# A fused attention and gated feed-forward kernel: wider PSUM regions, a copied hidden layer and a written-out order of work

## The chip, the cores and the metric

The kernel runs on one core of one Trainium2 chip. Its time is the device time of one execution in microseconds (us); lower is better. A core has TensorE (PE, matmuls; PEld are its weight loads), VectorE (DVE), ScalarE (ACT), GpSimd (POOL), and SyncE (SP), whose queue issues nearly all DMAs here. Each engine works through its own list of instructions in the order in which the program issues them, and waits there on semaphores for the others.

## The reference

Attention with a cluster mask, then a feed-forward layer (FFN), in float32:

```python
# q, k, v: (4 batches, 8 heads, 768 tokens, 64); centroids: (8, 16, 64)
q_assign = argmax(q_n @ c_n.T); k_assign = argmax(k_n @ c_n.T)   # nearest centroid, vectors normalised
mask = q_assign[:, :, :, None] == k_assign[:, :, None, :]
scores = where(mask, q @ k.T / 8, -1e9)
x = softmax(scores) @ v                       # as (3072 tokens, 512)
h = x @ w_in                                  # (3072, 1024)
e = exp(h - max(h)); solu = h * e / sum(e)
ln = (solu - mean(solu)) / sqrt(var(solu) + 1e-6) * g_ln
out = ln @ w_out                              # (3072, 512)
```

## The kernel before

**Attention.** The work is cut into 16 pairs of heads (4 batches by 4 pairs). For a pair, q and k are loaded (`load`, `load_tokens`), turned so that the head dimension lies on partitions (`turn` on DVE at L326; in batch 0 `turn_tokens` on PE at L303 and a copy), and cast into `qbig` and `kbig` (`cast`, L332 to L336). `clusters` (L346) multiplies with the centroids; `turn_back`, `assign_max`, `assign_hot` and `assign_turn` (DVE, L353 to L368) make one-hot rows, and `place` (L375, eight copies a pair) puts them beside the head dimension of `qbig` and `kbig`. With these rows a score gets 256 added where the clusters agree, so one exponential with a bias of -256 does mask and softmax numerator at once.

A unit is 256 (query, head) rows against 768 keys: 96 units in all, 24 a batch. Its scores fill three PSUM banks of 512 columns (`scores`, L458); each bank is exponentiated by one ACT instruction (`expo`, L463). Twelve matmuls (`values`, L475) multiply the result with v and a column of ones; `normalise` (L487, L498) divides. In batches 0 to 2 the units of a head follow one another for the first three pairs, and the last pair goes by blocks of 256 queries; a block of 128 tokens is complete for the FFN only when the last pair has reached it.

**FFN.** There are 24 blocks f of 128 tokens. For each: `turn_x` (a transposing DMA on SP, L506), `f_h` (eight matmuls, L539), `f_max` and `f_neg` (DVE, L546, L550), `f_exp` (two ACT instructions that read PSUM, L557), `f_u` (two DVE products e times h that read PSUM, L563), `f_turn` (transposing DMA), `f_bn` and `f_aggr` (DVE, L574, L578), `f_alpha` (four small POOL instructions, L584 to L590), `f_y` (eight matmuls, L600), `f_scale` (L606, L608), `f_out`. Before this, w_in is cast on POOL (L408), and w_out is summed over its rows and centred on DVE (L425 to L437).

**PSUM.** Scores have three banks in a ring, h three, the attention output one, everything else one. A bank of h is held until its product `f_u` is done.

**Order.** `Weave` holds every operation with an engine, a cost and a key, and `run` plays a list scheduler at build time: it takes the ready operation with the smallest key at the earliest time, and the instructions are issued in that order. `AWAY` moves single operations to another engine.

Of the kernel before, what the change touches and what calls it, by code (L numbers as in the profile page):

```python
# [13 lines left out]
AXY = mybir.AxisListType.XY  # L14
# [7 lines left out]
class Weave:  # L22
# [3 lines left out]
    FEED_KINDS = "tx ptx tu ptu hm h ng ex u bn ag al y sc ou".split()  # L26
    PAIR_KINDS = "ld tp xa xt ca lv cv cl tb mx oh ot pl bl".split()
    FEED = [-1, 2, 2.5, 4.5, 5, 4, 6.5, 11, 18, 7.5, 8, 12.5, 7.5, 21, 10, 15.5, 16.5, 10.5,
        4.5, 7.5, 1.5, 0.5, 2.5, -0.5]
    PAIR = [-27, 0, 1.5, -6, -9, -4.5, 0, -3, 19.5, -7.5, 1.5, -3, 21, 13.5, 21, 19.5]  # L30
    KIND = {'cv': -23.5, 'wi': -36.0, 'tb': -12.0, 'ca': 16.0, 'xa': 20.0, 'N': -1.0, 'tp':
        38.0, 'lg': 36.5, 'lo': -4.0, 'pl': -3.0, 'bl': 11.5, 'z': 35.5, 'xt': -1.0, 'lv': 1.5,
        'ce': -1.0, 'oh': -1.0, 'su': 0.5, 'ld': 5.0, 'li': 4.0, 'ot': -1.0, 'cl': 0.5, 'mx':
        0.5}
    AWAY = {}
    AWAY.update(dict.fromkeys("""
        ca0.0.1.0 ca0.0.1.1 ca0.1.0.0 ca1.1.1.0 ca1.2.1.0 ca1.3.0.1 ca2.1.0.0 ca2.1.0.1
        ca2.2.0.1 ca2.3.0.0 ca3.3.0.1 xa0.0.0 xa0.2.0 xa0.2.1 xt0.2.0 xt0.2.1 xt0.3.1
    """.split(), "ACT"))
    AWAY.update(dict.fromkeys("""  # L40
        bl3.2 bl3.3 pl0.0.0.1.0 pl0.0.0.1.1 pl0.0.1.1.0 pl3.0.0.1.1 pl3.2.0.0.0 pl3.2.0.1.0
        pl3.3.0.1.0 sc15 sc17 sc22
    """.split(), "DVE"))
    AWAY.update(dict.fromkeys("""
        bl0.0 ca0.0.0.0 ca0.0.0.1 pl0.0.0.0.0 pl0.0.0.0.1 pl0.0.1.0.0 pl0.0.1.0.1
        pl0.2.1.0.1 pl0.2.1.1.1
    """.split(), "POOL"))

    HOP = 0.17
    EPS = 0.12  # L50
    AHEAD = 2
    DEPTH = 4.0

    def __init__(self):
        self.ops, self.by = [], {}

    def add(self, name, eng, cost, key, fn, needs=(), after=(), take=None, give=None, move=0.0,
            bulk=False, lag=(0.5, 0.6)):
        assert name not in self.by, name
        key += self.later(name)  # L60
        self.by[name] = len(self.ops)
        self.ops.append(dict(name=name, eng=eng, cost=cost, key=key, fn=fn, needs=list(needs),
                             after=list(after), take=take, give=give, move=move,
                             bulk=bulk, lag=lag))

    def later(self, name):

        kind, rest = re.fullmatch(r"([A-Za-z]+)(.*)", name).groups()
        if kind in self.FEED_KINDS:
            return self.FEED[int(rest.split(".")[0])]  # L70
        if kind in self.PAIR_KINDS:
            b, p = rest.split(".")[:2]
            return self.PAIR[4 * int(b) + int(p)] + self.KIND.get(kind, 0)
        return self.KIND.get(kind, 0)

    def run(self):
        ops, by = self.ops, self.by
        n = len(ops)
        users = [[] for _ in range(n)]
        left = [0] * n  # L80
        for i, o in enumerate(ops):
            o["n"] = [by[x] for x in o["needs"]]
            o["a"] = [by[x] for x in o["after"]]
            left[i] = len(o["n"]) + len(o["a"])
            for j in o["n"] + o["a"]:
                users[j].append(i)
        start, end = [None] * n, [None] * n
        free, tokens, bus = {}, {}, 0.0
        ready = {}
        floor = [0.0] * n  # L90

        def open_(i):
            o = ops[i]
            floor[i] = max([end[j] + (self.HOP if ops[j]["eng"] != o["eng"] else 0.03)
                            for j in o["n"]] + [start[j] for j in o["a"]] + [0.0])
            ready.setdefault(o["eng"], []).append(i)

        for i in range(n):
            if not left[i]:
                open_(i)  # L100
        order = []
        while len(order) < n:
            best = None
            for e, lst in ready.items():
                t0 = free.get(e, 0.0)
                cand = []
                for i in lst:
                    tk = ops[i]["take"]
                    at = max(t0, floor[i])
                    if ops[i]["move"]:  # L110
                        at = max(at, bus - (self.AHEAD if ops[i]["bulk"] else self.DEPTH))
                    if tk is not None:
                        held = tokens.get(tk, 0.0)
                        if held is None:
                            continue
                        at = max(at, held + self.HOP)
                    cand.append((at, i))
                if not cand:
                    continue
                lo = min(c[0] for c in cand)  # L120
                at, i = min((c for c in cand if c[0] <= lo + self.EPS),
                            key=lambda c: (ops[c[1]]["key"], c[1]))
                if best is None or at < best[0]:
                    best = (at, i, e)
            at, i, e = best
            o = ops[i]
            ready[e].remove(i)
            start[i] = at
            free[e] = at + o["cost"]
            end[i] = at + o["cost"]  # L130
            if o["move"]:
                bus = max(end[i] + o["lag"][0], bus) + o["move"]
                end[i] = bus + o["lag"][1]
            if o["take"] is not None:
                tokens[o["take"]] = None
            if o["give"] is not None:
                tokens[o["give"]] = end[i]
            order.append(i)
            for j in users[i]:
                left[j] -= 1  # L140
                if not left[j]:
                    open_(j)
        self.start, self.end, self.order = start, end, order
        for i in order:
            ops[i]["fn"]()
# [3 lines left out]
def kernel(  # L149
# [25 lines left out]
    FF2 = 512  # L175
    n_ff2 = d_ff // FF2
    VS, VW = D + 2, D + 1

# [3 lines left out]

    const = ctx.enter_context(tc.tile_pool(name="const", bufs=1))
    big = ctx.enter_context(tc.tile_pool(name="big", bufs=1))
    wst = ctx.enter_context(tc.tile_pool(name="wst", bufs=4))
    ld = ctx.enter_context(tc.tile_pool(name="ld", bufs=8))
    xtp = ctx.enter_context(tc.tile_pool(name="xtp", bufs=6))
    pr = ctx.enter_context(tc.tile_pool(name="pr", bufs=3))
    vp = ctx.enter_context(tc.tile_pool(name="vp", bufs=3))
    ep = ctx.enter_context(tc.tile_pool(name="ep", bufs=9))  # L190
    mo = ctx.enter_context(tc.tile_pool(name="mo", bufs=2))
    sm = ctx.enter_context(tc.tile_pool(name="sm", bufs=4))
    ps_s = ctx.enter_context(tc.tile_pool(name="ps_s", bufs=3, space=bass.MemoryType.PSUM))
    ps_h = ctx.enter_context(tc.tile_pool(name="ps_h", bufs=3, space=bass.MemoryType.PSUM))
    ps_o = ctx.enter_context(tc.tile_pool(name="ps_o", bufs=1, space=bass.MemoryType.PSUM))
    ps_m = ctx.enter_context(tc.tile_pool(name="ps_m", bufs=1, space=bass.MemoryType.PSUM))
# [5 lines left out]
    def on(name, engine):  # L202
        return wv.AWAY.get(name, engine)

    R = 6
    qbig = [big.tile([P, 2, S], BF16, name=f"qbig{i}") for i in range(R)]
    kbig = [big.tile([P, 2, S], BF16, name=f"kbig{i}") for i in range(R)]
    v1 = [big.tile([P, 2, n_t, VS], BF16, name=f"v1_{i}") for i in range(R)]

    def slot(b, p):  # L210
        return (b * n_pair + p) % R

    def behind(b, p, what):

        i = b * n_pair + p - R
        if i < 0:
            return []
        b0, p0 = divmod(i, n_pair)
        ns = sorted({where[b0, 2 * p0 + hh, su] for hh in range(2) for su in range(n_t)})
        return [f"{what}{n}.{k}" for n in ns for k in range(n_k if what == "S" else 2)]  # L220

    SRC, DST = (q, k), (qbig, kbig)

    def rows(h):
        return slice(0, D) if h % 2 == 0 else slice(D, P)

    def hot_rows(hh):
        return slice(D, D + NB) if hh == 0 else slice(0, NB)

    def used(h):  # L230
        return slice(0, D + NC_) if h % 2 == 0 else slice(0, P)

    n_first = 2
    UNITS, GROUPS = [], []
    for b in range(B):
        if b < B - 1:
            for p in range(n_pair):
                a, c = 2 * p, 2 * p + 1  # L240
                if p < n_pair - 1:
                    hs = [[(h, s2) for s2 in range(n_t // 2)] for h in (a, c)]
                else:
                    hs = [[(a, s2), (c, s2)] for s2 in range(n_t // 2)]
# [40 lines left out]
    def by_token(b):  # L285

        return b < n_turned
# [665 lines left out]
```

## Time and profile before

| | |
|---|---|
| runs | 242.68, 243.94, 244.36 us; median 243.94 |
| span of the profiled execution | 238.8 us, 5.1 below the median |
| TensorE clock granted | 1.000 |
| PE, DVE, ACT, POOL busy | 219.9, 206.8, 204.9, 142.8 us |
| DMA | 38.61 MB |

The profile gives the profiled execution's span, from its first to its last instruction, and not its time; the runs' times include some 5 us around it. A busy time counts the union of the intervals in which an instruction is under way. Since a matmul is shown from issue to its last result, and the next one starts before that, PE's busy time is more than its work. For that the distance between the starts of instructions that follow one another without a wait is the better measure; it is called the pitch below.

### The profile page before, as it was taken

The page shows a single profiled execution, that of the slowest core. Times are in us where ns is not written, and L with a number is a line of the kernel's source. Part 1 is how long each engine was busy: PE and PEld are TensorE (multiplying, and loading weights), DVE is VectorE, ACT ScalarE, POOL GpSimd, SP SyncE. Part 2 cuts the span into 40 slices and gives each one's busy share as a digit, 9 for nine tenths or more (in the row PEclk, how much of TensorE's full clock was granted, in tenths as well). Part 3 has the DMA queues.
Part 4 walks back from the last instruction along what each step waited for, and adds up shares of the span by engine and source line. Part 5 has one row for each costly group of instructions (what it writes and reads, how often), then busy time and mean ns, then how long its engine had stood idle before and what let it go on. Part 6 is the DMA issues. An engine that isn't in the chain of part 4 may idle for free.

```text
span 238.8 us, 6759 instructions
## 1 busy us (share of the span) xinstructions
PE 219.9 (92%) x2384; PEld 147.5 (62%) x2384; DVE 206.8 (87%) x427; ACT 204.9 (86%) x428; POOL 142.8 (60%) x328
## 2 busy tenths in 40 slices
PE   0969999999999999899899999999999999999983
PEld 0646775675655667666566677657667776747441
DVE  4468699999999899999899999998979779999991
ACT  2569998999788999999899999988989998969461
POOL 4983888996075386898948648898802510310331
PEclk9999999999999999999999999999999999999999
DMA  7999988988599898989789989873535154558422
GB/s 203 273 275 219 255 306 226 183 123 180 98 156 202 166 221 166 207 169 212 138 179 180 204 144 165 214 186 96 69 88 50 48 113 110 72 152 154 91 88 88
DMA packets 133217, 38.61 MB, mean 162 GB/s; under 512 B 124472, under 2 KB 128576, under 8 KB 133184
## 3 DMA queue, kind: packets, MB, share of 16 engines
q1 hardware_dynamic: 131616, 37.80, 76.9%
q10 hardware_dynamic: 1568, 0.39, 0.7%
q8 instruction: 18, 0.29, 0.5%
q14 instruction: 15, 0.12, 0.2%
HBM read 23.11 MB, written 6.29 MB: 123 GB/s over the span
## 4 chain that ended last, share of the span: by engine, by line
PE 63%; DVE 10%; ACT 8%; POOL 7%; issue 6%; DMA 5%; ACTq 0%; DVEq 0%; POOLq 0%
PE sps L458 17%; PE yps L600 14%; PE hps L539 14%; PE ops L475 11%; ACT e L463 6%; PE csc L346 4%; DMA xT<-x 2%; DVE w_out_c L437 2%; PE tps L303 2%; DMA uT<-u 2%; DVE hm L546 2%; POOL kbig L336 1%; DVE qbig L375 1%; POOL qbig L334 1%; ACT e_sb L557 1%
## 5 line engine op out<-in xcount | busy, mean ns | idle before, releaser
L463 ACT ACTIVATE e<-sps 128x512 bf16<-128x512 f32 x288 | 148.8, 624 | 10.7 <-PE sps L458 10.1
L458 PE MATMUL sps<-qbig,kbig 80*128 80x256 bf16 (+3 forms) x648 | 101.5, 262 | 5.4 <-POOL qbig L375 2.2
L458 PEld LDWEIGHTS <-kbig 80*128 80x128 bf16 (+1 forms) x648 | 58.5, 121 | 24.6 <-issue 9.9
L475 PEld LDWEIGHTS <-e 128*128 128x128 bf16 x1152 | 57.2, 98 | 20.5 <-issue 3.8
L475 PE MATMUL ops<-v,e 128*128 128x65 bf16 x1152 | 65.5, 194 | 1.0 <-DVE x L498 0.6
L539 PE MATMUL hps<-w_in_sb,xT 128*128 128x512 bf16 x192 | 53.2, 379 | 1.4 <-DMA xT<-x 0.7
L600 PE MATMUL yps<-w_out_c,uT 128*128 128x512 bf16 x184 | 45.4, 379 | 1.1 <-DVE qbig L375 0.7
L557 ACT ACTIVATE e_sb<-hps,nmax 128x512 bf16<-128x512 f32 x48 | 32.9, 700 | 3.1 <-DVE nmax L550 3.1
L546 DVE TENSOR_REDUCE hm<-hps 128x1 f32<-128x512 f32 x48 | 31.9, 676 | 3.2 <-PE hps L539 2.8
L563 DVE TENSOR_TENSOR u<-e_sb,hps 128x512 bf16<-128x512 bf16 x48 | 31.7, 679 | 2.7 <-ACT e_sb L557 2.5
L375 POOL COPY kbig<-oht 32x192 f32<-32x192 f32 x57 | 20.9, 366 | 21.8 <-DVE oht L368 19.5
L574 DVE BATCH_NORM_STATS2 bs<-u 128x6 f32<-128x512 bf16 x48 | 31.6, 678 | 0.0
L600 PEld LDWEIGHTS <-uT 128*128 128x128 bf16 x192 | 17.9, 98 | 17.7 <-DMA uT<-u 1.2
L336 POOL TENSOR_SCALAR kbig<-xt 64x768 bf16<-64x768 f32 x28 | 23.4, 837 | 2.7 <-DVE xt L313 1.3
L334 POOL CAST qbig<-xt 64x768 bf16<-64x768 f32 x25 | 21.5, 860 | 5.5 <-ACT xt L311 4.5
L539 PEld LDWEIGHTS <-xT 128*128 128x128 bf16 x192 | 17.1, 97 | 10.4 <-issue 1.1
L588 POOL TENSOR_TENSOR esq<-esq,mv 128x1 f32<-128x1 f32 x24 | 4.6, 192 | 30.1 <-DVE mv L578 29.1
L326 DVE STREAM_TRANSPOSE xt<-raw 128x768 f32<-128x768 f32 x24 | 22.1, 950 | 0.1
L375 POOL COPY qbig<-oht 32x192 f32<-32x192 f32 x50 | 18.8, 376 | 2.6
L498 DVE TENSOR_TENSOR x<-ops,den 128x384 bf16<-128x384 f32 (+1 forms) x37 | 18.6, 504 | 1.3
L606 ACT ACTIVATE y<-yps,alpha 128x512 f32<-128x512 f32 x20 | 13.9, 695 | 5.7 <-POOL alpha L590 2.9
L389 POOL CAST v<-vf 128x384 bf16<-128x384 f32 x32 | 16.3, 534 | 3.9 <-DMA vf<-in_v_dram 3.4
(75 smaller groups left out, 191.9 us busy)
## 6 DMA issues: line engine op xcount, KB each, us to landing
vf<-in_v_dram SPq DMA_DIRECT2D x16, 384.0 KB, 4.2
out_dram<-y SPq DMA_DIRECT2D x24, 256.0 KB, 2.3
raw<-in_q_dram SPq DMA_DIRECT2D x48, 96.0 KB, 3.6
raw<-in_k_dram SPq DMA_DIRECT2D x48, 96.0 KB, 2.7
w_st<-in_moe_w_in_dram SPq DMA_DIRECT2D x4, 512.0 KB, 5.6
w_g<-in_moe_w_out_dram SPq DMA_DIRECT2D x4, 512.0 KB, 8.0
raw<-in_q_dram SPq DMA_DIRECT2D x7, 192.0 KB, 4.1
raw<-in_k_dram SPq DMA_DIRECT2D x7, 192.0 KB, 4.4
```

The source lines that it names most:

```text
L334: nc.gpsimd.tensor_copy(dst[r, hh, :], xt[r])
L336: nc.gpsimd.tensor_scalar(dst[r, hh, :], xt[r], scalar1=inv_C, scalar2=1.0, op0=Alu.mult, op1=Alu.mult)
L375: (nc.vector if e == "DVE" else nc.gpsimd).tensor_copy(dst, src)
L458: nc.tensor.matmul(sps_[n, k][:, c0:c0 + w], kbig[z][u, h % 2, keys], qbig[z][u, h % 2, q0:q0 + w])
L463: nc.scalar.activation(es[n, k][:], sps_[n, k][:], Act.Exp, scale=exp_scale, bias=-exp_scale)
L475: nc.tensor.matmul(opss[g][:, s, :VW], es[n, k][:, c0:c0 + P], v1[slot(b, h // 2)][:, h % 2, kt, :VW], start=(kt == 0), stop=(kt == n_t - 1))
L539: nc.tensor.matmul(ff[f, "h", f2][:], xTs[f][:, dc, :], w_in_sb[:, dc, f2 * FF2:(f2 + 1) * FF2], start=(dc == 0), stop=(dc == n_dc - 1))
L546: nc.vector.tensor_reduce(ff[f, "hm"][:, f2:f2 + 1], ff[f, "h", f2][:], axis=AX, op=Alu.max)
L557: nc.scalar.activation(ff[f, "e"][:, f2, :], ff[f, "h", f2][:], Act.Exp, bias=ff[f, "nmax"][:], accum_out=ff[f, "esum"][:, f2:f2 + 1])
L563: nc.vector.tensor_tensor(ff[f, "u"][:, f2, :], ff[f, "e"][:, f2, :], ff[f, "h", f2][:], op=Alu.mult)
L574: nc.vector.bn_stats(ff[f, "bs"][:, f2, :], ff[f, "u"][:, f2, :])
L600: nc.tensor.matmul(ff[f, "y"][:], ff[f, "uT"][:, fc, :], w_out_c[:, fc, :], start=(fc == 0), stop=(fc == n_fc - 1))
```

## The change

It is a rewrite of most of the kernel; the arithmetic is that of before. In words:

- Batch 0: pair 0 goes first, all of it; then blocks of 256 queries of the other three pairs follow one another. Its tokens are loaded as (partition, six tokens), one DMA a tensor and pair, and the output rows are written accordingly.
- The eight PSUM banks are fixed tiles: two regions of two banks for scores (`sb`), two banks for h (`hb`), one each for `ob` and `mb`. Two units form a stretch of 3072 columns, cut into regions of 1024; a region gets one exponential. The first two units keep 512. 147 exponentials take the place of 288.
- `f_max` copies -h from PSUM to SBUF and gathers its minimum in the same instruction, bank by bank; `f_neg` is gone. `f_exp` is one ACT instruction of 1024 columns and `f_u` one product of 1024 columns, both from SBUF; the last f keeps halves. 18 of the 24 products, and half of the last, go to POOL.
- From pair 2 on, one-hot rows are made for two pairs at once, and `place` writes them for both heads of both pairs: 40 instructions in place of 128. Nine are on ACT, ten on DVE. Pair 0 is done in two halves.
- The row sum of w_out goes to PE (eight matmuls in column tiles and one to fold); its centring is split between POOL and DVE.
- `f_scale` is on DVE for ten f instead of three.
- `Weave.run` issues the names in `ORDER`, a fixed list of 1,610, in place of the scheduler.

```diff
-                    key=lambda c: (ops[c[1]]["key"], c[1]))
...
+ORDER = """
+ld0.0.0 lg ld0.0.1 ld0.1.0 ld0.1.1 cx cy cz cp tp0.0.0.0 xa0.0.0 cb tp0.0.0.1 gt tp0.0.1.0 lv0.0
+ld0.2.0 ld0.2.1 ld0.3.0 ld0.3.1 gk xt0.0.0 xa0.0.1 cl0.0 ca0.0.0.0.0 ca0.0.1.0.0 tb0.0 mx0.0 oh0.0
+ot0.0 pl0.0.1.0 ca0.0.1.1.0 tp0.0.1.1 tp0.1.0.0 xt0.0.1 xa0.1.0 ca0.0.1.1.1 cl0.0.1 pl0.0.0.1
+tb0.0.1 pl0.0.0.0 tp0.1.0.1 xt0.1.0 tp0.1.1.0 xa0.1.1 tp0.1.1.1 xt0.1.1 cl0.1 ca0.0.0.0.1
...
+        for name in ORDER:
+            o = self.ops[name]
...
+            o["fn"]()
...
+AWAY.update(dict.fromkeys("""
+    ca0.0.0.0.0 ca0.0.0.1.1 ce1 ce5 ce7 pl0.0.1.1 u1.0 u11.0 u12.0 u13.0 u14.0 u15.0 u16.0
+    u18.0 u19.0 u2.0 u21.0 u22.0 u23.1 u3.0 u4.0 u5.0 u6.0 u7.0 u8.0
+""".split(), "POOL"))
...
+    sb = [psum.tile([P, 2, BANK], F32, name=f"sb{i}") for i in range(2)]
+    hb = psum.tile([P, 2, BANK], F32, name="hb")
+    ob = psum.tile([P, BANK], F32, name="ob")
+    mb = psum.tile([P, BANK], F32, name="mb")
...
+        if b == 0:
+            for s2 in range(n_t // 2):
+                side(b, 0, s2)
+            for s2 in range(n_t // 2):
+                for p in range(1, n_pair):
+                    side(b, p, s2)
...
+            w = BANK if n < 2 * n_fine else 2 * BANK
...
+        nc.scalar.activation(es[r][:, :w], src, Act.Exp, scale=exp_scale, bias=-exp_scale)
...
-        nc.vector.tensor_reduce(ff[f, "hm"][:, f2:f2 + 1], ff[f, "h", f2][:], axis=AX, op=Alu.max)
...
+        nc.vector.tensor_scalar(ff[f, "h"][:, f2 * BANK:(f2 + 1) * BANK], hb[:, f2], scalar1=-1.0,
+                                scalar2=nmax[:, f2 - 1:f2] if f2 else 3.0e38, op0=Alu.mult,
+                                op1=Alu.min, accum_out=nmax[:, f2:f2 + 1])
...
+        nc.scalar.activation(ff[f, "e"][:, cols(f, f2)], ff[f, "h"][:, cols(f, f2)], Act.Exp,
+                             bias=ff[f, "nmax"][:, n_ff2 - 1:], scale=-1.0,
+                             accum_out=ff[f, "esum"][:, f2:f2 + 1])
...
+        (nc.vector if e == "DVE" else nc.gpsimd).tensor_tensor(
+            ff[f, "u"][:, cols(f, f2)], ff[f, "e"][:, cols(f, f2)], ff[f, "h"][:, cols(f, f2)],
+            op=Alu.mult)
...
+        src = (asg[t, "oht"][r, :w * L].bitcast(F32).rearrange("p (g s) -> p g s", g=w)
+               .unsqueeze(2).to_broadcast([NB, w, 2, L // 2]))
+        dst = big_[D:HOT, pp:pp + w, :, c0 + x * L:c0 + (x + 1) * L].bitcast(F32)
...
+    def sum_w_out(x):
+
+        for c in range(4):
+            fc = 4 * x + c
+            nc.tensor.matmul(hb[c * NB:(c + 1) * NB, 1], g_wide[:, fc, :], w_g[:, fc, :],
+                             start=(x == 0), stop=(x == n_fc // 4 - 1),
+                             tile_position=(0, c * NB))
```

In `ORDER`, S and E are scores and exponential of a region, V the values of half a unit, N the division, h, hm, ex, u, tu, y, sc, ou the steps of an FFN block, ld and lv loads, ca and cv casts, cl, tb, mx, oh, ot, pl the steps of the one-hot rows. E40 is about the 25th unit's last exponential.

More of the change, by code (lines that the diff above doesn't have):

```diff
@@ L61, in add @@
[L61 to L74, printed above, removed]
@@ L76, in run @@
-    def run(self):
[L77 to L121, printed above, removed]
-                            key=lambda c: (ops[c[1]]["key"], c[1]))
[L123 to L145, printed above, removed]
@@ L222 @@
[L222 to L228 removed]
+        return AWAY.get(name, engine)
+    sb = [psum.tile([P, 2, BANK], F32, name=f"sb{i}") for i in range(2)]
+    hb = psum.tile([P, 2, BANK], F32, name="hb")
+    ob = psum.tile([P, BANK], F32, name="ob")
+    mb = psum.tile([P, BANK], F32, name="mb")
+    R2, R = 3, 6
+    qbig = [big.tile([HOT, 2, 2, S], BF16, name=f"qbig{i}") for i in range(R2)]
```

1132 lines of the change are left out of this document (665 added, 467 removed).

## The prediction

> **What bounds the kernel now.** First the page: span and busy shares.
>
> ```profile
> span 238.8 us, 6759 instructions
> ...
> PE 219.9 (92%) x2384; PEld 147.5 (62%) x2384; DVE 206.8 (87%) x427; ACT 204.9 (86%) x428; POOL 142.8 (60%) x328
> ```
>
> PE is busy for 92% of the span, but its busy time counts overlaps, so I take its work by pitch. The timeline of PE shows stretches without a wait (start, duration, instructions):
>
> ```profile
> 121.83 1.89 PE L600 MATMUL yps<-w_out_c,uT 128*128 128x512 bf16 x8
> 123.56 0.38 PE L458 MATMUL sps<-qbig,kbig 80*128 80x256 bf16 x2
> ...
> 123.97 0.61 PE L458 MATMUL sps<-qbig,kbig 80*128 80x256 bf16 x4
> 124.42 0.35 PE L475 MATMUL ops<-v,e 128*128 128x65 bf16 x6
> 124.61 1.46 PE L539 MATMUL hps<-w_in_sb,xT 128*128 128x512 bf16 x6
> 125.91 0.62 PE L458 MATMUL sps<-qbig,kbig 80*128 80x256 bf16 x4
> ```
>
> ```profile
> 26.46 0.85 PE L346 MATMUL csc<-xt,c_bd 128*32 128x384 f32 x8
> 27.25 0.36 PE L475 MATMUL ops<-v,e 128*128 128x65 bf16 x6
> ...
> 28.30 0.49 PE L303 MATMUL tps<-ident_f,raw 128*128 128x128 f32 x3
> 28.63 0.38 PE L458 MATMUL sps<-qbig,kbig 80*128 80x256 bf16 x2
> ```
>
> Eight FFN matmuls of 512 columns take 123.56 - 121.83 = 1.73 us (0.216 each), four score matmuls of 256 columns 0.45, six value matmuls 0.19, the eight of `clusters` 0.79, three transposes 0.33. With the counts of the groups of instructions:
>
> ```profile
> L458 PE MATMUL sps<-qbig,kbig 80*128 80x256 bf16 (+3 forms) x648 | 101.5, 262 | 5.4 <-POOL qbig L375 2.2 <-ACT e L463 0.9
> ...
> L475 PE MATMUL ops<-v,e 128*128 128x65 bf16 x1152 | 65.5, 194 | 1.0 <-DVE x L498 0.6 <-ACT e L463 0.2
> ...
> L539 PE MATMUL hps<-w_in_sb,xT 128*128 128x512 bf16 x192 | 53.2, 379 | 1.4 <-DMA xT<-x 0.7 <-DVE w_out_c L437 0.5
> ```
>
> 288 banks of 512 score columns are 288 x 0.225 = 64.8; values 1152 / 6 x 0.19 = 36.5; h and as many for y 384 x 0.216 = 83.1; 16 `clusters` 12.6; 48 transposes 5.3; the rest about 2.2. **PE's work is 204.5 us, so 34.3 of the span is idle.** Where? The stages, cut at the first exponential, near the first FFN matmul and at the last scores (columns: stage, length, busy time and count of PE, PEld, DVE, ACT, POOL, clock, DMA share, GB/s):
>
> ```profile
> 0.00:14.15 14.15, 6.32 (x34) 4.45 (x35) 7.47 (x26) 4.61 (x7) 10.02 (x32) 1.00 0.98 241
> 14.15:57.50 43.35, 40.85 (x522) 28.42 (x521) 36.80 (x75) 41.38 (x84) 35.09 (x56) 1.00 0.93 223
> 57.50:220.00 162.50, 158.90 (x1752) 108.25 (x1750) 149.43 (x301) 150.72 (x321) 92.27 (x224) 1.00 0.78 146
> 220.00:238.80 18.80, 13.84 (x85) 6.41 (x82) 13.07 (x29) 8.15 (x18) 5.42 (x18) 1.00 0.32 96
> ```
>
> and PE's groups of the first two stages together:
>
> ```profile
> L458 PE MATMUL sps<-qbig,kbig 80*128 80x256 bf16 (+1 forms) x156 | 28.0, 271 | 4.1 <-POOL qbig L375 2.2
> L475 PE MATMUL ops<-v,e 128*128 128x65 bf16 x298 | 17.2, 194 | 0.6 <-DVE x L498 0.6
> L303 PE MATMUL tps<-ident_f,raw 128*128 128x128 f32 x48 | 8.5, 313 | 0.0
> L346 PE MATMUL csc<-xt,c_bd 128*32 128x384 f32 x48 | 6.8, 549 | 0.0
> ```
>
> That is 156 x 0.1125 + 298 x 0.0317 + 48 x 0.11 + 6 x 0.79 + 1.2 = 38.2 us of work in 57.5. Before the first exponential there are at most 14.15 - 6.3 = 7.8 us of busy-time idle; by pitch some 10. So the second stage has some 9 idle, the third 162.5 - (204.5 - 38.2 - 13.8) = 10.0, the last at least 18.8 - 13.8 = 5.0. The second stage is ACT's: 41.4 of 43.35 busy, and PE has no FFN work to fill in, since its first such matmul starts at 58.2:
>
> ```profile
> L539 PE MATMUL hps<-w_in_sb,xT x192: 376/379/390, 58.2 to 227.5; 128*128 128x512 bf16 x192
> ```
>
> The granted clock is 1.00 throughout. In the third stage PE is at 98% and ACT at 93%, DVE at 92%; it is PE's, with ACT and DVE close behind. **An edit pays only where it takes PE idle time away.**
>
> **PE's work after** is 204.5 plus the row sum of w_out: eight f32 matmuls in column tiles, like two `clusters` widened from 384 to 512 columns, 2 x 0.79 x 512 / 384 = 2.1. The fold stands for the old mean. So 206.6.
>
> **Start.** The chain that ended last opens so (start, us, what):
>
> ```profile
> 5.60 0.48 PE cps L659
> ...
> 8.63 1.75 PE csc L346 x8
> ...
> 14.15 3.53 ACT e L463 x7
> ```
>
> From the norms' end at 5.60 to the first exponential are 8.55 us: transposes, `clusters`, four DVE steps, placing. The new list does these steps for half of pair 0's tokens, which at half the width would save near half of the roughly 4.1 that `clusters` and the DVE steps take. But ahead of S0.0 it also puts the transposes of pair 1: nine half-tensor transposes (0.33), three `clusters` (two of half size) and the centroids', 5 us of PE. From 5.6 that gives 11.0 if no load is late, and 14.15 if the loads of pair 1 eat the gain. I take E0 at 12.0, nearer the first, since the PE rows are known and only the loads are not.
>
> **Second stage, E0 to E40** (about 25 units; before, PE had done 156 / 2 = 78 banks of scores, 26 units, at 57.5). ACT's rows:
>
> ```profile
> 90.70 3.03 ACT L463 ACTIVATE e<-sps 128x512 bf16<-128x512 f32 x6
> 93.57 0.75 ACT L606 ACTIVATE y<-yps,alpha 128x512 f32<-128x512 f32 x1
> ```
>
> ```profile
> L463 ACT ACTIVATE e<-sps 128x512 bf16<-128x512 f32 x288 | 148.8, 624 | 10.7 <-PE sps L458 10.1 <-PE ops L475 0.2
> ...
> L557 ACT ACTIVATE e_sb<-hps,nmax 128x512 bf16<-128x512 f32 x48 | 32.9, 700 | 3.1 <-DVE nmax L550 3.1
> ...
> L332 ACT ACTIVATE qbig<-xt 64x768 bf16<-64x768 f32 x7 | 5.9, 845 | 0.1
> ```
>
> Six exponentials take 93.57 - 90.70 = 2.87, a pitch of 0.478. One of 1024 isn't shown. It costs at most two, 0.956, and at least what 768 columns do, 0.845 less the 0.146 by which 0.624 lies over its pitch, so 0.70. Between 512 and 768 columns the duration rises by 0.863 ns a column; 0.478 + 512 x 0.863 = 0.92, which I take. The Trainium skill (ScalarE: Activation LUTs, What ACT_TABLE_LOAD costs) gives 186 ns plus 0.833 ns a column, less 93 where instructions follow one another: 0.520 for 512, where this trace has 0.478, and 0.946 for 1024. By it the stage is 0.9 longer, an estimate.
>
> Counting the list between E0 and E40: ACT 6 x 0.478 + 34 x 0.92, two FFN exponentials (each two of 0.57 less one start, about 1.1) and seven small ones of about 0.5, 39.7. PE 74 score halves, 47 halves of a unit's values, 13 half-banks of h, four `clusters`, seven transposes and the w_out sum, 39.4. DVE and POOL come to 37 and 34. So where ACT alone was full, two engines are now level, and PE carries 45.1 us of work by E40 against 38.2 before. Before, the stage had 84 ACT instructions: some 77 exponentials, 36.8, and seven others of about 0.53, so 40.5 of 43.35, and the coupling cost 2.9; with two level engines I take 4.3 (0 if the list fits, 8 if as much is lost as PE's idle now). **E40 at 12.0 + 39.7 + 4.3 = 56.0**, with 6.9 more PE work behind it.
>
> **Third stage.** ACT loses 0.036 for each of 107 more exponentials, 3.9, and per FFN block about 0.2; seven `f_scale` go to DVE. On DVE and POOL:
>
> ```profile
> L546 DVE TENSOR_REDUCE hm<-hps 128x1 f32<-128x512 f32 x48 | 31.9, 676 | 3.2 <-PE hps L539 2.8
> L563 DVE TENSOR_TENSOR u<-e_sb,hps 128x512 bf16<-128x512 bf16 x48 | 31.7, 679 | 2.7 <-ACT e_sb L557 2.5
> ...
> L408 POOL CAST w_in_sb<-w_st 128x1024 bf16<-128x1024 f32 x4 | 4.1, 1036 | 0.1
> ...
> L608 DVE TENSOR_SCALAR y<-yps,alpha 128x512 f32<-128x512 f32 x3 | 2.2, 749 | 0.5 <-POOL esq L588 0.5
> ```
>
> ```profile
> L375 POOL COPY kbig<-oht x57: 337/343/807, 12.9 to 188.2; 32x192 f32<-32x192 f32 x57
> ...
> L375 DVE COPY qbig<-oht x14: 247/252/1207, 13.1 to 186.5; 32x192 f32<-32x192 f32 x14
> ```
>
> DVE loses 48 products of 0.679, 32.6, and keeps five and a half of 1024; at twice the row, 7.5. The copy with minimum is nearest to L608 (f32 from PSUM, a scalar per partition), 0.749 against 0.676 for the reduction: plus 3.5. Seven more scalings add 5.2. Net 16 fewer, and the w_out sum goes besides. POOL loses most of its copies: 18 wide ones of 768 columns take the place of 72 of 192 at 0.343. A wide one costs at most four narrow ones, 1.37, and at least three quarters of the cast of 1024, 0.78; I take 0.85, near the row that is nearest in width. Against it stand 18 and a half products of 1024 with two inputs. The trace has no such POOL instruction: at least one pass as the cast of 1024, 1.04; at most two passes, 2.07. I take 1.6. The list from E40 to E120 then has PE 106.0, ACT 97.7, DVE 88, POOL 82, so PE's neighbours move away. I take the third stage's idle of 10.0 for PE waiting on their results, and half of it, 5.0, to stay (2 to 10.0). The tail keeps its order (h, y and the last block's chain), 5.0.
>
> The Trainium skill (GPSIMD Engine Reference, Elementwise) says that a GpSimd product of two tensors takes about 2.6 cycles an element at 1.2 GHz; that is 2.2 us here, an estimate, and it puts POOL at 88.7 in that stretch, still under PE. No run here shows it; by it rival 2 below would need 21 us of waits instead of 23, and I would give it 0.12 instead of 0.10.
>
> **New waits.** h has two banks instead of three, but each comes free after one DVE pass, where it was held through reduction, exponential and product; behind `f_max` stand DVE's transposes and `normalise`, and PE's next h. The copy goes to a staging tile of which there are three, so `f_max` of block f now waits for the product of f - 3, which is mostly POOL's. A score region waits for the exponential two regions back; between these lies one exponential, 0.92, for 0.45 of score matmuls, so ACT is fed as long as PE holds no more than about 0.4 of other work in between; before, two exponentials of 0.478 lay there. On SP a transpose of u waits for POOL's product, and the loads behind it in the list wait along. The front half of the last product pair goes by DVE, the rear by POOL: at most one pass of 512 more in the tail, 0.4.
>
> A further edge of moving `f_u` is the DVE copies: the same copy took 247 ns at best and 1207 at worst beside POOL work. With longer POOL instructions such stretches could reach 2 us, for some 20 DVE instructions whose inputs are all in SBUF, 20 us at most if every one lost half a stretch; with 16 us and the w_out sum off DVE I leave it at nothing on the path.
>
> **The sum.** 56.0 + (206.6 - 45.1) + 5.0 + 5.0 = **227.5 us of span**, and with the 5.1 that the median lies above the profiled span, 232.6; I say 232.6 against 243.94. SP's queue issues the same loads, transposes and stores, some with one DMA where there were two, so DMA work stays; the loads have to come earlier by the time gained, for which DMA has room in the third stage, at a share of 0.78, and little in the second, at 0.93.
>
> **Rivals.**
>
> 1. *The idle time is only exchanged.* Two level engines lose 6.8 in the second stage, and the third keeps its 10.0: 58.5 + 161.5 + 15.0 + 5.1 = 240.1. For it: the list is fixed and each engine waits in order. Against: ACT and DVE get 4% and 8% lighter. Chance 0.15.
> 2. *POOL's queue becomes the bound (slower).* A product there waits in order for its exponential, and the casts and one-hot rows of the next pair stand behind it; a late product also holds the copy of f + 3 on DVE, and through its bank PE. Waits of POOL before:
>
> ```profile
> POOL kbig L375 <- DVE oht L368: 19.5, 7, 7.3
> ...
> POOL es L584 <- ACT e_sb L557: 16.0, 5, 8.4
> ```
>
> Five waits for an exponential took 16.0, 3.2 each. From E40 to E120 eleven products at 2.07 make POOL's work 87; 19.5 for one-hot rows remain; eleven waits of 3.2 add 35. That is 142 against PE's 106 + 4. If half of the excess is hidden by overlapping waits, 16 are lost: 249. It decides once POOL's waits there exceed 23. Against: most products come when their exponential is long done, as the list places them several regions later. Chance 0.10.
> 3. *A wide exponential costs as two.* Then ACT is 1.3 longer in the second stage and off PE's path later: 234. Chance 0.08.
> 4. *The list fits better than I allow.* Coupling 1, third stage 2 idle: 52.7 + 161.5 + 7.0 + 5.1 = 226.3. Chance 0.10.
>
> **How the numbers follow.** The forecast has the remaining 0.57, between 228 and 237. About 1%, 2.4 us, is what a measurement can tell from no change. Faster by more: forecast, 3, 4 and two thirds of 1, 0.85; within 1%: the rest of 1, 0.05; slower: 2, 0.10. The range reaches from rival 4 to rival 1, with a microsecond about them: 225 to 241; that leaves out 2 and a little of the others.
>
> **What would show it.** Right: the first exponential near 12 us, the first FFN matmul before 50, PE's idle time by pitch near 21, the 1024-column pitch at 0.92, products on POOL at 1.6, POOL waiting less than 23 us between E40 and E120. Wrong: PE waiting for POOL casts or placings in the third stage, weight loads held by uT transposes, or an exponential near 1 us. A third stage with 10 us idle speaks for rival 1.

## The result: slower, and the profile after

The change makes the kernel slower: 267.58 us (median, 266.96 to 269.17) against 243.68 measured beside it; the ratio is 1.0998, with a 95% interval of 1.0937 to 1.1058. The forecast was 232.6 us, 11.3 below the kernel before; the measured time is 23.9 above it. Executions of one kernel differ by up to some 3%; the ratios leave the long ones out and the medians do not, so where the two differ, the ratios count.

Span and busy times, from the page of the kernel after:

```profile
span 265.4 us, 6301 instructions
...
PE 224.4 (85%) x2378; PEld 150.7 (57%) x2408; DVE 179.9 (68%) x381; ACT 198.5 (75%) x247; POOL 166.2 (63%) x233
```

DVE fell by 26.9 us, ACT by 6.4, POOL rose by 23.4: the work moved as intended. By the prediction's count PE's work is still near 206 us, so some 59 us of the span are idle, where it was 34. By stage, cut again near the first exponential, the first FFN matmul and the last scores (stage, length, busy time and count of PE, PEld, DVE, ACT, POOL, clock, DMA share, GB/s):

```profile
0.00:17.90 17.90, 10.66 (x59) 5.68 (x60) 8.17 (x30) 6.62 (x13) 7.26 (x23) 1.00 0.93 216
17.90:50.70 32.80, 28.84 (x370) 20.43 (x368) 23.80 (x45) 29.39 (x37) 23.12 (x33) 1.00 0.80 204
50.70:240.60 189.90, 166.12 (x1838) 115.78 (x1865) 136.21 (x280) 152.45 (x181) 124.09 (x159) 0.97 0.68 134
240.60:265.40 24.80, 18.81 (x120) 8.84 (x119) 11.77 (x29) 10.02 (x17) 11.74 (x21) 1.00 0.34 104
```

The third stage is where it went: 189.9 us, of which PE is busy for 166.1. Before, it was busy for 158.9 of 162.5. No engine is full there, so the engines wait for one another. The groups of instructions that matter here (busy time, mean ns of one | idle time ahead of them and what ended it):

```profile
L574 ACT ACTIVATE e<-sb 128x1024 bf16<-128x1024 f32 (+1 forms) x147 | 142.2, 1004 | 36.5 <-PE sb L564 32.5 <-PE ob L584 2.5
L656 PE MATMUL hb<-w_in_sb,xT 128*128 128x512 bf16 x176 | 51.4, 386 | 20.8 <-DVE w_st L666 17.8 <-POOL w_in_sb L503 1.9 <-issue 0.2
L689 POOL TENSOR_TENSOR u<-e_sb,w_st 128x1024 bf16<-128x1024 bf16 (+1 forms) x19 | 39.8, 2094 | 24.1 <-ACT e_sb L682 17.8 <-issue 5.2 <-POOL kbig L468 0.9
...
L666 DVE TENSOR_SCALAR_CACHE_REDUCE w_st<-hb,nmax 128x512 f32<-128x512 f32 x24 | 17.8, 743 | 10.9 <-PE hb L656 10.0 <-PE sb L564 0.7
L666 DVE TENSOR_SCALAR_CACHE_REDUCE w_st<-hb 128x512 f32<-128x512 f32 x24 | 16.3, 681 | 15.3 <-PE hb L656 11.5 <-ACT e L574 3.3 <-POOL kbig L399 0.5
```

One row stands out on PE, the engine that counts: the h matmuls (L656) waited 20.8 us, 17.8 of them for `f_max` (L666). Before, the same matmuls (L539) waited 1.4. In the third stage PE has no matmul under way for 23.8 us, and 17.8 of these are that wait. And `f_max` in turn waited 21.5 us for h matmuls (10.0 and 11.5): each waits for the other. The timeline of PE and DVE shows one such place, the longest (start, duration, instructions, in brackets the wait before):

```profile
190.23 0.75 DVE L666 TENSOR_SCALAR_CACHE_REDUCE w_st<-hb,nmax 128x512 f32<-128x512 f32 x1 [1.12 <-PE hb L656]
...
192.42 2.70 DVE L443 TENSOR_TENSOR oh<-cst,mx 128x768 bf16<-128x768 f32 x1
...
195.15 0.59 PE L656 MATMUL hb<-w_in_sb,xT 128*128 128x512 bf16 x2
...
198.93 0.69 DVE L666 TENSOR_SCALAR_CACHE_REDUCE w_st<-hb 128x512 f32<-128x512 f32 x1
199.55 0.08 DVE L666 DVE_READ_ACCUMULATOR w_st<-hb 128x1 f32 x1
199.69 0.59 PE L656 MATMUL hb<-w_in_sb,xT 128*128 128x512 bf16 x2 [3.72 <-DVE w_st L666]
```

In the list this is `hm15.1 ... h16.0.0 ... h16.0.1 ... hm16.0 ... h16.1.0`. The `f_max` that reads `nmax` is that of the second half, so at 190.23 DVE reads bank 1 of h, and by 191 bank 1 is free. PE then fills bank 0 (to 195.7), and its next matmul of h, `h16.1.0`, writes bank 1. Nothing in the data holds it. It starts at 199.69, right after the `f_max` of bank **0**. That one was late because DVE was busy without a break from 192.4 on, with a one-hot comparison of 2.70 us and the steps listed behind it. Is that so everywhere? In the timeline of after, none of the 176 recorded h matmuls begins while an `f_max` runs; in that of before, 37 of 192 do.

### The profile page after: what moved, and what is told of

Its sections match the earlier page's. It is cut to its first block, busy times and chain, and to the rows that moved or that the text cites. A ratio compares the mean times of both kernels' runs of the same rounds, so it can differ in the third digit from the quotient of the medians.

```text
span 265.4 us, 6301 instructions
## 1 busy us (share of the span) xinstructions
PE 224.4 (85%) x2378; PEld 150.7 (57%) x2408; DVE 179.9 (68%) x381; ACT 198.5 (75%) x247; POOL 166.2 (63%) x233
## 4 chain that ended last, share of the span: by engine, by line
PE 36%; DVE 24%; POOL 12%; ACT 10%; SPq 7%; issue 6%; DMA 4%; DVEq 0%; POOLq 0%; ACTq 0%
PE hb L656 10%; PE sb L564 9%; ACT e L574 6%; DVE w_st L666 6%; PE mb L727 5%; SPq L382 5%; PE ob L584 4%; PE mb L420 4%; DVE bs L700 3%; DVE oh L443 3%; DVE xt L389 3%; POOL u L689 2%; PE hb L366 2%; POOL alpha L723 2%; POOL w_out_c L547 2%
## 5 line engine op out<-in xcount | busy, mean ns | idle before, releaser
L574 ACT ACTIVATE e<-sb 128x1024 bf16<-128x1024 f32 (+1 forms) x147 | 142.2, 1004 | 36.5 <-PE sb L564 32.5
L564 PE MATMUL sb<-qbig,kbig 96*128 96x256 bf16 (+3 forms) x648 | 94.6, 265 | 4.1 <-ACT e L574 3.2
L564 PEld LDWEIGHTS <-kbig 96*128 96x128 bf16 (+1 forms) x648 | 62.1, 121 | 32.3 <-issue 15.2
L656 PE MATMUL hb<-w_in_sb,xT 128*128 128x512 bf16 x176 | 51.4, 386 | 20.8 <-DVE w_st L666 17.8
L584 PE MATMUL ob<-v,e 128*128 128x65 bf16 x1152 | 56.9, 195 | 1.9 <-DVE x L606 1.5
L689 POOL TENSOR_TENSOR u<-e_sb,w_st 128x1024 bf16<-128x1024 bf16 (+1 forms) x19 | 39.8, 2094 | 24.1 <-ACT e_sb L682 17.8
L727 PE MATMUL mb<-w_out_c,uT 128*128 128x512 bf16 x170 | 47.1, 381 | 0.8 <-DVE y L735 0.2
L656 PEld LDWEIGHTS <-xT 128*128 128x128 bf16 x192 | 18.0, 99 | 32.9 <-issue 23.8
L682 ACT ACTIVATE e_sb<-w_st,nmax 128x1024 bf16<-128x1024 f32 (+1 forms) x25 | 27.8, 1111 | 6.6 <-DVE w_st L666 5.8
L399 POOL TENSOR_SCALAR kbig<-xt 64x768 bf16<-64x768 f32 (+1 forms) x30 | 23.8, 794 | 13.2 <-ACT xt L375 7.2
L397 POOL CAST qbig<-xt 64x768 bf16<-64x768 f32 (+1 forms) x29 | 24.6, 853 | 7.0 <-DVE xt L377 3.1
L666 DVE TENSOR_SCALAR_CACHE_REDUCE w_st<-hb 128x512 f32<-128x512 f32 x24 | 16.3, 681 | 15.3 <-PE hb L656 11.5
L666 DVE TENSOR_SCALAR_CACHE_REDUCE w_st<-hb,nmax 128x512 f32<-128x512 f32 x24 | 17.8, 743 | 10.9 <-PE hb L656 10.0
```

The lines of the kernel that those rows point to most:

```text
L397: (nc.vector if e == "DVE" else nc.gpsimd).tensor_copy(dst, src)
L564: nc.tensor.matmul(reg[:, c:c + wd], kb[u, pp, h % 2, keys], qb[u, pp, h % 2, su * P:su * P + wd])
L574: nc.scalar.activation(es[r][:, :w], src, Act.Exp, scale=exp_scale, bias=-exp_scale)
L584: nc.tensor.matmul(ops[:, s, :VW], es[r][:, c0:c0 + P], v1[index[b, h // 2] % R][:, h % 2, kt, :VW], start=(kt == 0), stop=(kt == n_t - 1))
L656: nc.tensor.matmul(hb[:, f2], xTs[f][:, dc, :], w_in_sb[:, dc, f2 * BANK:(f2 + 1) * BANK], start=(dc == 0), stop=(dc == n_dc - 1))
L666: nc.vector.tensor_scalar(ff[f, "h"][:, f2 * BANK:(f2 + 1) * BANK], hb[:, f2], scalar1=-1.0, scalar2=nmax[:, f2 - 1:f2] if f2 else 3.0e38, ...
```

## The experiments

Three theories stood at the start. **A**: h's two banks are the two halves of one tile, `hb`, and the program's waits go by the tile. Then every h matmul waits for every `f_max` listed ahead of it, and the reverse, whichever bank they touch. **B** (rival 2 of the prediction): POOL's products, 2.09 us each on average (2.15 for the 18 of full width), are late. **C**: SP's queue and the loads are late. **D** came along with A: whatever joins two banks loses, the wide exponentials too.

### Two tiles for h

```diff
-    hb = psum.tile([P, 2, BANK], F32, name="hb")
+    hb = [psum.tile([P, BANK], F32, name=f"hb{i}") for i in range(2)]
```

and `hb[f2][:]` in the place of `hb[:, f2]` throughout. List, engines and banks stay.

> The two banks of h become two tiles instead of the two halves of one; nothing else is changed, the list neither. Theory A (one tile): in the trace of the changed kernel PE's matmuls into h never begin before the last f_max listed ahead of them has ended, also where that f_max reads the other bank, and f_max waits likewise for matmuls of the other bank. The 17.8 us that L656 waits for L666 then go, and some of what DVE waits for h: 245 us (240 to 250), and the first exponential up to 1 us earlier, since the transposes of batch 0 use the same banks. Theory B (POOL's products of 2.09 us are late) and theory C (SP's queue and the loads are late): no wait that they speak of is touched, 265 to 268.

Measured: 244.19 us, beside 242.83 for the kernel before; ratio 1.0023, 0.9971 to 1.0075. **Making two tiles of one gives back 22.5 of the 23.9 us lost.** From the groups of this run and its timeline (its trace is of an execution of 245.84 us):

```profile
L656 PE MATMUL hb<-w_in_sb,xT 128*128 128x512 bf16 x176 | 50.4, 379 | 3.9 <-DVE w_st L666 1.7 <-POOL w_in_sb L503 1.2 <-DMA xT<-x 0.2
```

```profile
174.14 0.59 PE L656 MATMUL hb<-w_in_sb,xT 128*128 128x512 bf16 x2
175.65 0.73 DVE L666 TENSOR_SCALAR_CACHE_REDUCE w_st<-hb,nmax 128x512 f32<-128x512 f32 x1
175.67 0.38 PE L656 MATMUL hb<-w_in_sb,xT 128*128 128x512 bf16 x1
```

The wait for `f_max` fell from 17.8 us to 1.7. At 175.67 PE writes one bank while DVE reads the other from 175.65 on; 38 of the 176 matmuls now begin during an `f_max`. A holds, and B and C had expected no change.

### The products on DVE, with one tile and with two

```diff
-    ca0.0.0.0.0 ca0.0.0.1.1 ce1 ce5 ce7 pl0.0.1.1 u1.0 u11.0 u12.0 u13.0 u14.0 u15.0 u16.0
-    u18.0 u19.0 u2.0 u21.0 u22.0 u23.1 u3.0 u4.0 u5.0 u6.0 u7.0 u8.0
+    ca0.0.0.0.0 ca0.0.0.1.1 ce1 ce5 ce7 pl0.0.1.1
```

> All products of the FFN on DVE, none on POOL; same list, h still one tile. B: POOL loses 39.8 us of work and the products come after 1.2 us instead of 2.1; 255 to 262. A: DVE gets 19 products of about 1.2 us, 23 us, in the queue in which f_max stands, and every f_max still holds both banks: 272 to 282. C: no change, 265 to 270.

> The edits of the two runs above together. A: the products on DVE still push f_max back by up to 23 us in all, but only the bank's own matmuls wait: 250 to 260, so slower than with two tiles alone. B: faster than the run with two tiles alone, by 3 us or more.

Measured, in one execution each: 281.22 with one tile, 253.69 with two. Taking the slow products off POOL makes both worse, by 13.6 and 9.5 us, in the ranges that A had given; against B, they were better placed on POOL. From the groups of the first of the two:

```profile
L654 PE MATMUL hb<-w_in_sb,xT 128*128 128x512 bf16 x176 | 52.4, 392 | 22.4 <-DVE w_st L664 19.5 <-POOL w_in_sb L501 1.9 <-issue 0.2
...
L687 DVE TENSOR_TENSOR u<-e_sb,w_st 128x1024 bf16<-128x1024 bf16 (+1 forms) x25 | 30.4, 1224 | 3.3 <-ACT e_sb L680 3.2
```

A product on DVE takes 1.22 us instead of 2.09, but it stands in the queue of `f_max`. PE waits there 19.5 us, only 1.7 more than the 17.8 before, so this wait is the smaller part of the 13.6. The granted clock fell from 0.980 to 0.956 over the span, which is up to 7 us of lost clock (279.4 x 0.044 against 265.4 x 0.020); the rest lies in short waits of PE for other results of DVE and POOL. That the loss came out in A's range is therefore in part luck.

### The cause put into the kernel before

If A is right it is a rule and not an accident of this list, and the kernel before, which has three h banks as three tiles, should lose by joining them. Besides h, the transposes of batch 0, the mean of w_out and some of the y results use these banks.

```diff
+    h_all, h_at = ps_h.tile([P, 3, 512], F32, name="hps"), [0]
+
+    def h_bank(w):
+        h_at[0] += 1
+        return h_all[:, h_at[0] % 3, :w]
...
-        tps[b, p, i, hf] = ps_h.tile([P, HALF], F32, name="tps", tag="hps")
+        tps[b, p, i, hf] = h_bank(HALF)
...
-            ff[f, "h", f2] = ps_h.tile([P, FF2], F32, name="hps", tag="hps")
+            ff[f, "h", f2] = h_bank(FF2)
```

> The kernel before, with its three h banks made one tile of three banks, used in turn as they were; order, widths and engines stay. If waiting goes by the tile (theory A), every matmul into h waits for all f_max, exponentials and products listed ahead of it, and each of these for the matmuls listed ahead: far more than the 21 to 23 us that two banks cost after the change, 260 to 300. If it goes by the bank, 243.

Measured, in one execution: 290.64 us beside 243.28, 47 us more. From its groups:

```profile
L545 PE MATMUL hps<-w_in_sb,xT 128*128 128x512 bf16 x172 | 53.4, 399 | 33.6 <-DVE u L569 20.0 <-DVE hm L552 5.7 <-ACT e_sb L563 5.5
```

The h matmuls, which waited 1.4 us before, wait 33.6, for products, `f_max` and exponentials. None of the 172 recorded ones begins during an `f_max`, where 37 of 192 did with three tiles.

### Narrow exponentials, with four score tiles and with two

The wide exponentials need two banks in one tile as well. The first run goes back to 512 columns with four score tiles and ten buffers for the results; the second joins these by twos again and changes nothing else.

```diff
-    sb = [psum.tile([P, 2, BANK], F32, name=f"sb{i}") for i in range(2)]
+    sb = [psum.tile([P, BANK], F32, name=f"sb{i}") for i in range(4)]
...
-    n_fine = 1
+    n_fine = n_units
```

> Two tiles of h, and besides the exponentials back to 512 columns, each with its own score bank (four tiles instead of two), ten buffers for their results; the list with two halves in the place of each wide exponential. The wide form saves 2 x 0.478 - 0.904 = 0.05 us each, 7 us of ACT's time in all, but couples two banks. If ACT's time counts (A says that with two tiles PE waits for little else than ACT and DVE): 1 to 4 us slower than with two tiles alone. If the coupling of the banks costs more than that, which is theory D (whatever joins two banks loses): 1 to 4 us faster.

> As the run with two tiles of h and 512-column exponentials (241.4 us), but the four score banks are again two tiles of two banks each; width, list and buffers stay. If joined banks cost (theory D), the scores of a bank wait for the exponential of its neighbour, as with the wide form, and each exponential costs 0.478 where the wide one costs 0.452 for as many columns: 244 to 248, no faster than the wide form with two tiles of h (244.2). If the narrow form was faster for its ten buffers or its finer steps alone, 240 to 243.

Measured: 241.41 with four tiles (ratio 0.9857, 0.9785 to 0.993) and 245.80 with two (1.0079, 1.0027 to 1.0131); the wide form had 244.19. D holds: joining costs 4.4 us by the medians and 2.2%, 5.4 us, by the ratios to the kernel before, whose intervals lie apart. The row of ACT's waits for scores, with four tiles and then with two (us, times, longest):

```profile
ACT e L580 <- PE sb L570: 4.8, 12, 1.3
```

```profile
ACT e L580 <- PE sb L570: 11.7, 25, 1.7
```

Whether 1024 columns are worth anything with joined tiles is not settled: 244.19 against 245.80, with intervals that overlap. Narrow ones with four tiles beat both: the intervals lie apart, though that version has only four executions, from 237.95 to 242.46. From here on the runs build on that version.

### The first exponential moved ahead

Pair 1's nine steps `tp0.1.0.0` to `cl0.1` stood ahead of `S0.0`, between steps of pair 0:

```diff
-z2 S0.0 tp0.2.0.0 S1.0 S2.0 E0 cv0.0.0
+z2 S0.0 S1.0 S2.0 E0 tp0.1.0.0 xa0.1.0 tp0.1.0.1 xt0.1.0 tp0.1.1.0
+xa0.1.1 tp0.1.1.1 xt0.1.1 cl0.1 tp0.2.0.0 cv0.0.0
```

> As the run with two tiles of h and narrow exponentials on four tiles (241.4 us), but the transposes and clusters of pair 1 stand behind the first three score matmuls in the list instead of ahead of them. If the late first exponential (16.0 us there, 13.9 before the change) costs as much at the end: the first exponential near 14, the total 239 to 240. If the second stage has to wait for pair 1 anyway: the first exponential near 14 and the total 241 to 244.

Measured: 245.12 (ratio 1.0075, 1.003 to 1.0119), 3.7 us more than without the move and 2.2% by the ratios; that is above both expected ranges. ACT's first exponentials with the move:

```profile
15.08 0.57 ACT L581 ACTIVATE e<-sb 128x512 bf16<-128x512 f32 x1
19.18 1.09 ACT L581 ACTIVATE e<-sb 128x512 bf16<-128x512 f32 x2
```

and without it:

```profile
16.20 2.52 ACT L580 ACTIVATE e<-sb 128x512 bf16<-128x512 f32 x5
19.54 0.59 ACT L580 ACTIVATE e<-sb 128x512 bf16<-128x512 f32 x1
```

The first one comes 1.1 us earlier, but the second, at 16.20 + (2.52 - 0.59) / 4 = 16.7 without the move, comes 2.5 later. An early first exponential alone was worth nothing here. That the later start of the steady row is what cost the time fits these rows, but no run tests it alone.

### Shorter products

With `u`, `e` and `h` for the block's tiles:

```diff
-            nc.gpsimd.tensor_tensor(u, e, h, op=Alu.mult)
+            nc.gpsimd.tensor_scalar(u, e, scalar1=h[:, 0:1], scalar2=1.0, op0=Alu.mult, op1=Alu.mult)
```

> Again on two tiles of h and narrow exponentials on four tiles (241.4 us). The 19 products on POOL become a scaling of the exponential by the first column of h: it waits for the same two tiles and writes the same one, but does one pass instead of two; the product with the other 1023 columns is left out. Expected 1.05 us each instead of 2.16, so 21 us less for POOL. If POOL's products hold the kernel up (theory B): 5 us faster or more, 236 or less. If they are mostly hidden, as the list places them: 1 to 4 us faster, 237.5 to 240.5.

This kernel leaves out most of the product, so it serves for its time alone. Measured: 236.08 us (0.9739, 0.9673 to 0.9805), 5.3 less by the medians; from its groups:

```profile
L696 POOL TENSOR_SCALAR u<-e_sb,w_st 128x1024 bf16<-128x1024 bf16 (+1 forms) x19 | 22.0, 1159 | 21.3 <-ACT e_sb L688 17.8 <-issue 1.1 <-DMA raw<-in_q_dram 1.1
```

By the ratios, 0.9739 against 0.9857, the gain is 1.2%, 2.9 us, and the intervals overlap. So 19 us less on POOL are worth some 3 to 5 us, and the run does not decide between the two expectations. Nor is the gain POOL's queue alone: the three wide one-hot comparisons on DVE that run beside a product became 2.9 us shorter in all (1.84, 2.10 and 2.70 us with the long products, 1.01, 1.07 and 1.68 with the short ones).

### A new list with measured durations

The list notes 1.56 us for a product on POOL and 1.2 for a centring of w_out there; the traces have 2.15 at full width and, in two instructions, 2.08.

```diff
-ld0.0.0 lg ld0.0.1 ld0.1.0 ld0.1.1 cx cy cz cp tp0.0.0.0 xa0.0.0 cb tp0.0.0.1 gt tp0.0.1.0 lv0.0
+cx ld0.0.0 lg z4 z1 z3 ld0.0.1 sg cy z5 cz z2 cp cb ld0.1.0 tp0.0.0.0 tp0.0.0.1 ld0.1.1 xa0.0.0 gt
...
```

> As the run with two tiles of h and narrow exponentials on four tiles (241.4 us): the same operations on the same engines, in another order. The list was written anew with the durations that the traces show in place of those noted in the kernel: 2.15 us for a product on POOL (noted 1.56), 2.1 and 0.95 for a centring of w_out on POOL and DVE (1.2 and 0.66), 0.72 for an f_max (0.66), slower transposes and clusters ahead of the first exponential. If the rest of the loss is that the list was made for other durations: a part of the 5.3 us that the short products gave, the same again for the centrings, and 2 to 3 us at the start, where the first exponential should come near 13 instead of 16: 231 to 237. If the rest is in the operations (more work on POOL, two h banks, SP's queue): 239 to 243.

> The same, and besides 44 small operations on other engines (casts, one-hot copies, blanks, scalings; three products move between DVE and POOL). If engines are well enough balanced already: within 1 us of the run before it. If POOL's load is what is left: 1 to 3 us faster than it.

Measured: 237.04 (0.9726, 0.9671 to 0.9781) and, with the 44 moves, 236.06 (0.97, 0.9648 to 0.9752). Both beat the kernel before and the change. The new list alone is worth 4.4 us by the medians over the version with four score tiles and 1.3%, some 3 us, by the ratios, whose intervals only just lie apart; its median is 0.04 above the range expected if the list was at fault, and 2 below the other. The moves add nothing that can be told. The stages of the new list:

```profile
0.00:16.00 16.00, 9.22 (x59) 5.90 (x60) 9.35 (x31) 9.02 (x18) 9.21 (x29) 1.00 0.91 220
16.00:50.00 34.00, 33.06 (x440) 24.14 (x440) 29.80 (x53) 32.64 (x66) 27.20 (x31) 1.00 1.01 230
```

PE and ACT are both nearly full from 16 to 50 us (33.1 and 32.6 of 34), and the DMA engines too, at 1.01. Theory C had no run of its own; that DMA share says that the loads can hardly come faster there, but whether the second stage waits for them was not tried.

## Why the prediction was wrong, point by point

**The step that failed** is in "New waits": "h has two banks instead of three, but each comes free after one DVE pass". It takes the banks for what the program waits for. The program waits for tiles, and `hb` is one tile, so a bank came free only after the `f_max` of its neighbour too. PE, `f_max` and everything between two `f_max` in DVE's order formed one chain through all 24 blocks. The run with two tiles prices this at 22.5 us, and no term of the sum had it. Joining the banks of the kernel before cost 47 us, so it is no accident of this list. The code shown said it: `hb` is made in one line, as `[P, 2, BANK]`, where the kernel before took a new tile for each half.

The chip did not need these waits, as the run with two tiles shows: 38 of its h matmuls begin during an `f_max`, and `f_max` is no slower for it (mean 677 and 741 ns against 681 and 743 with one tile). The Trainium skill (PSUM — Partial Sum Buffer, Summary: rules for kernel authors) says that while a matmul runs one should read a different bank. The runs agree.

**The idle time of the third stage**, forecast as 5.0 with an upper bound of 10.0, is the term that this made wrong most. From E40 to the end the sum has 161.5 + 5.0 + 5.0 = 171.5 us. E40 began at 69.64 and the span ended at 265.44, so it took 195.8, and by the prediction's own count of PE's work 34.3 of them are idle, where 10.0 were forecast. With two tiles for h it took 178.7.

**The start** was forecast at 12.0 us; the first exponential came at 17.98:

```profile
17.98 0.60 ACT L574 ACTIVATE e<-sb 128x512 bf16<-128x512 f32 x1 [0.36 <-PE sb L564]
```

The 5 us of PE work ahead of it were priced with a row from later in the run, three transposes in 0.33. The same three at the start, and later at the pace of that row:

```profile
8.11 0.90 PE L366 MATMUL sb<-ident_f,raw 128*128 128x128 f32 x3
...
11.14 0.85 PE L366 MATMUL hb<-ident_f,raw 128*128 128x128 f32 x3
...
17.20 0.49 PE L366 MATMUL hb<-ident_f,raw 128*128 128x128 f32 x3
```

So the early transposes take nearly twice as long. The row for `clusters` in the prediction's own quote of the start, 1.75 us for eight where 0.85 was taken later, had shown it. Of the rest, 1.4 us come from the transposes' use of `hb`: with two tiles the first exponential is at 16.56. With four score tiles it is at 16.20, and the new list brings it to 13.18:

```profile
16.56 0.60 ACT L574 ACTIVATE e<-sb 128x512 bf16<-128x512 f32 x1 [0.36 <-PE sb L564]
```

```profile
13.18 0.60 ACT L580 ACTIVATE e<-sb 128x512 bf16<-128x512 f32 x1
```

**The second stage**: E40 was forecast at 56.0. The exponentials of after by stretch (busy time and count):

```profile
17.98:50.70 32.72, 25.90 (x30) 1.00 0.79 203
50.70:69.40 18.70, 10.67 (x11) 0.91 0.88 176
```

Thirty and eleven, with one that lies across 50.70 and counts in both: these are E0 to E39, and E40 begins at 69.64. The first FFN matmul came at 50.9 against "before 50", but the last 18.7 us hold only some ten exponentials. From E0 to E40 it took 51.7 us where 39.7 + 4.3 = 44.0 were forecast, so the coupling was 12.0. The chain through `hb` is the smaller part: with two tiles it still took 48.8. In the stretch PE waited 3.2 us for exponentials, 1.9 for the cast of w_in on POOL and 1.5 for `f_max`; what made the rest is open.

**The wide exponential** was right: forecast 0.92 a pitch; two take 1.91 here, so 0.91 with the last one's 1.00, and over all 62 pairs without a wait between them the median is 0.92.

```profile
113.85 1.91 ACT L574 ACTIVATE e<-sb 128x1024 bf16<-128x1024 f32 x2
```

Rival 3, that it costs as two, is out. What it bought does not show in the time: on joined score tiles, wide and narrow exponentials cannot be told apart, and narrow ones on four tiles were faster.

**The product on POOL** was mis-sized: 1.6 taken between 1.04 and 2.07, measured 2.15 at full width, above the upper bound. The estimate from the Trainium skill (GPSIMD Engine Reference, Elementwise), 2.2, was nearer. With the tiles apart, the run that shortens it by 1.0 us gains 3 to 5 us; by that the half microsecond missed here would be worth 1.5 to 3, an estimate.

**The stretched DVE copies** were left "at nothing on the path". The one-hot comparison of 2.70 us, where the shortest of its width takes 0.92, ran from 192.42 on, and POOL's product beside it from 192.16:

```profile
192.16 2.14 POOL L689 TENSOR_TENSOR u<-e_sb,w_st 128x1024 bf16<-128x1024 bf16 x1
```

It held an `f_max` and through it PE; so this does reach the path where DVE's order is on it. POOL's product ends at 194.30 and the comparison, which reads two SBUF tiles, 0.82 later. Two more comparisons of this width overlap a product in this trace; they take 1.81 and 1.43 us and end 0.82 after it too. In the run with one tile for h and the products on DVE, the same three take 1.20, 0.95 and 0.90. The Trainium skill (SBUF — State Buffer, Who interferes with whom) says that DVE and GpSimd share a pair of SBUF ports under an exclusive lock, and that a DVE instruction with two SBUF inputs contends with a GpSimd instruction that reads SBUF. These rows agree.

**The rivals.** Rival 2 had the sign and a time of 249. POOL's waits between E40 and E120 (69.4 to 190.8) came to 27 us, above the 23 from which it was to decide, but 5.2 of these have no cause that the profile shows, and without them they are 22. Its mechanism was not the cause in any case: with two tiles for h the products stayed on POOL as they were, and 22.5 of the 23.9 us came back. Rival 1, idle time only exchanged, is near what remained once the tiles were apart: 244.19, where it said 240.1. Against its 6.8 lost in the second stage and 15.0 idle behind it, the trace of that run has 48.8 - 39.7 = 9.1 and 178.7 - 161.5 = 17.2, and the start 4.6 late besides, which is no part of rival 1. **The tail**, 5.0 idle, came out at 24.8 - 18.8 = 6.0; but it was 24.8 us long, since more FFN work was left over. The copy with minimum was right, 743 ns where 749 was taken, and DVE fell by 26.9 us, where the prediction had 16 and the w_out sum besides. **The 5.1 us** between span and median, which the sum adds and the table before the change puts down to time around the execution, are two things: in most executions the time is 1.8 us above its own span (267.22 and 265.4 here) and never more than 3.4, so the rest is that the profiled execution was a short one. That the forecast, 232.6, is near what was reached with the tiles apart, narrow exponentials and a list made for them, 236 to 237, does not bear it out: that is another kernel, and the 4 us between are not accounted for.

## What to carry to other kernels

Before a bank, buffer or half is counted as free, look at which tile it belongs to: what the program waits for is the tile, and in an order written out by hand a wait that the planner did not know turns into a chain. In the profile it shows as two groups that each wait for the other while neither engine is full, and in the timeline as two kinds of instructions that never overlap. A saving on an engine should not be counted until one has checked what the resource that it joins or holds was doing for the others.

## What the runs showed of the hardware

Matmuls at the start of the run took nearly double, 0.85 to 0.90 us for three transposes up to about 12 us and 0.49 later. The granted clock in the stage rows stands at 1.00 there, but the trace's record of the clock only begins at 12.7 us, just when the transposes become faster, and the rows count the time ahead of it as full. The Trainium skill (TensorE: Matmul & The Clock Gate, Part 1: The HAM clock gate) tells of half the clock until the array has been busy for about 3.4 us. The factor agrees; the slow pace lasted some 7 us from the first matmul at 5.3, with 0.65 us of PE idle in between.

The granted clock also fell behind some of PE's waits. In the trace of after it is 0.50 in three stretches of 3.4 us within the third stage, from 53.69, 132.20 and 200.46 on. Waits of the h matmuls of 1.9, 1.9 and 3.7 us had ended up to 0.8 us ahead of each; a wait of 3.2 us that ended at 239.95 had no such stretch behind it before the span was nearly over. In the new list's two stages shown above it stays at 1.00. So idle time of PE can cost more than itself: three stretches at half the clock are 5 us of PE's pace, an estimate.
